# The bias stage of an attention and mixture kernel written into the one order of steps

## The chip, the cores and the metric

The kernel runs on one core of a Trainium2 chip. The metric is device time of one execution in microseconds (us). The core has five engines with a queue each: TensorE (PE, with its weight loads as PEld), VectorE (DVE), ScalarE (ACT), GpSimd (POOL) and SyncE (SP), which issues the transfers here. Each queue is worked off in order, and an instruction that waits holds up all that stand behind it on its engine.

## The reference, cut to what matters

Attention of 8 batches and 8 heads over 576 positions with 64 columns a head, with a bias that a small network makes of the positions, and then a soft mixture of 8 experts on what comes out:

```python
scores = scale * np.matmul(q, k.transpose(0, 1, 3, 2))
psi_rel = np.log1p(np.abs(pos[:, None] - pos[None, :]))
psi_i = np.log1p(np.maximum(pos[:, None], 1.0))
x = (psi_rel / psi_i)[..., None]
h = np.maximum(x @ w1 + b1, 0.0)          # 32 hidden units
scores = scores + (h @ w2).transpose(2, 0, 1)[None]
attn = softmax(scores);  out = np.matmul(attn, v)
# then a soft mixture: logits = out @ phi, softmax over tokens and over slots, 8 experts
```

The bias is the same for all batches: 576 x 576 values for each of 8 heads.

## The kernel before, in words

**The bias stage.** It comes first, and has 36 jobs (`jobs`), each for 16 rows of the bias and all heads. Job i needs four feature tiles f (128 partitions, 304 to 576 columns), each one instruction that scales a table and cuts it at zero: on DVE (line 324), but the first of the four on ACT in five jobs of six (line 321), so 114 on DVE and 30 on ACT. PE multiplies the four by the second layer's weights `wbd` side by side in the array (line 345), in pieces that meet at the diagonal and at a bank's end (three pieces, twelve products, in most jobs). ACT adds a constant and keeps the 591 columns as a tile e (line 349); SP stores e in DRAM (line 350, `bias_m`, and `bias_r` for the last four jobs). `bias_group()` writes one job, with the features of three jobs ahead (`AHEAD`), in the order of the row numbers. f and e tiles share 25 buffers (`W1N`, tag w); the PSUM banks are a fixed pair of four in turn. Then `load_bias` reads the bias of one pair of heads back, skewed, in five tiles (line 381): c = 0 to 3 need the stores of jobs 8c to 8c+7, and c = 4 (`br`, six transfers) those of jobs 32 to 35.

**The attention units.** A unit u is one pair of heads in one batch; there are 32. A unit has row blocks p (0 to 3, and 4 in even units for the rest rows of two units). The steps, by their names in the order: `Sp.n/u` are score products for both heads and one half of the columns (lines 465, and 470 for p = 4; two PSUM banks), `tp.hn/u` adds the bias and takes the running minimum on DVE (line 485, frees one bank), `ep.h/u` is the exponential on ACT (line 494), `mp` the reciprocal of the sums on DVE (lines 501, 502), `np.h` the division on POOL (line 400), `Tp` and `Rp` turn the result on PE (line 449), `cp` and `cRp` copy that out of PSUM (line 403; a plus sign after a name puts the copy on DVE, otherwise on ACT), `Mc` multiplies by v (line 571), `xc` copies that out, `xs` stores it, `lq`, `lv` and `b` load. Units 24 to 31 also hold the mixture's steps.

**The order.** `ORDER` is one written list of all steps of the units. `then` looks up each step's place, the steps are sorted by it, and each engine's queue is what the list gives it. PSUM banks of a step are the ones idle for longest at that place in the list (`Banks`). The bias stage isn't in the list of before: its calls stand ahead of it, and the compiler's own scheduler orders their transfers.

In the text, "the cut" is the place of `S0.0/5`, from which the lists of before and after are the same to the end.

Of the kernel before, what the change touches and what calls it, by code (L numbers as in the profile page):

```python
# [57 lines left out]
S1.0/8 S1.1/8 t1.10/8 n2.1/7 t1.00/8 R3/7 S3.0/8 t1.11/8 T2/7 cR3/7 xs/6 t1.01/8 e0.0/8 T3/7 t3.00/8 t3.10/8 m0/8
S3.1/8 c3/7+ xs/5 e1.0/8 e1.1/8 M0/7 m1/8 t3.01/8 S4.0/8 n0.1/8 c2/7 S4.1/8 e3.0/8 n0.0/8 t3.11/8 e3.1/8 x0/7+ t4.00/8
n1.0/8 t4.10/8 n1.1/8 R1/8 cR1/8 T0/8 t4.01/8 m3/8 n3.0/8 c0/8 t4.11/8 S2.0/8 lv/8 w0/8 e4.0/8 e4.1/8 S0.0/9 t2.10/8  # L60
t2.00/8 S2.1/8 S0.1/9 t2.11/8 t2.01/8 e2.1/8 w1/8 m4/8 n4.0/8 e2.0/8 n4.1/8 T1/8 n3.1/8 c1/8 M1/7 t0.00/9 R4/8 t0.10/9
T3/8 t0.11/9 t0.01/9 m2/8 cR4/8 e0.0/9 n2.1/8 T4/8 n2.0/8 x1/7+ S1.0/9 T2/8 c3/8+ c4/8 R3/8 S3.0/9 t1.00/9 t1.10/9
cR3/8+ c2/8 lq/10 S3.1/9 t3.00/9 t3.10/9 S1.1/9 S2.0/9 S2.1/9 t3.01/9 e0.1/9 t3.11/9 e3.1/9 M1/8 m0/9 n0.1/9 t2.10/9
e3.0/9 t2.00/9 t1.01/9 t1.11/9 e1.0/9 e1.1/9 lq/11 n0.0/9 t2.11/9 m3/9 e2.1/9 n3.0/9 m1/9 t2.01/9 n1.1/9 n1.0/9 n3.1/9
e2.0/9 M0/8 T0/9 x0/8 x1/8 m2/9 R1/9 S0.0/10 n2.0/9 S0.1/10 cR1/9 c0/9 t0.00/10 t0.10/10 T1/9 lv/9 w0/9 t0.01/10
# [4 lines left out]
e2.1/10 w1/10 m4/10 n4.0/10 e2.0/10 n4.1/10 T1/10 n3.1/10 c1/10 M1/9 t0.00/11 R4/10 t0.10/11 T3/10 t0.11/11 t0.01/11  # L70
m2/10 cR4/10 e0.0/11 n2.1/10 T4/10 n2.0/10 x1/9+ S1.0/11 T2/10 c3/10+ c4/10 R3/10 S3.0/11 t1.00/11 t1.10/11 cR3/10+
# [140 lines left out]
def body(ctx, tc, qk, v, wcol, phi, mw1, mw2, tabh, consth, out, outr):  # L212
# [95 lines left out]

    feats = {}

    def bias_feats(i):
        bases, scales, _ = jobs[i]
        fb = [None] * 4
        relu = [False] * 4
# [820 lines left out]
```

## Time and profile before

| what | us |
|---|---|
| runs | 597.39, 593.42, 595.76 (median 595.76) |
| profiled execution | 595.49 |
| its span, first to last instruction | 593.7 |
| around the span | 1.8 |

The profiled execution lies 0.27 us below the median, so a difference worked out in its trace is taken from its own time. The runs spread over 4 us. Times below count from the span's start. A busy share says how long an engine had something in flight; matmuls overlap, and their ends are modelled.

### The profile page before, as it was taken

How to read it: one execution, taken by the hardware profiler on the slowest of the kernel's cores; microseconds unless marked ns; L12 is line 12 of the kernel's file. 1: busy time of each engine (PE TensorE's matmuls, PEld its weight loads, DVE VectorE, ACT ScalarE, POOL GpSimd, SP SyncE). 2: the span in 40 equal slices, each digit the busy share in tenths (PEclk: the TensorE clock that was granted, in tenths of full speed). 3: DMA queues.
4: the chain of work that ended last, by engine and by line, in shares of the span. 5: the costliest groups of instructions: out<-in, count | busy, mean ns of one | idle time of the engine just before them, and what ended most of it. 6: DMA issues, size and time to landing. Idle time of an engine off the chain costs nothing.

```text
span 593.7 us, 19374 instructions
## 1 busy us (share of the span) xinstructions
PE 564.0 (95%) x7391; PEld 368.8 (62%) x7391; DVE 464.3 (78%) x1813; ACT 451.0 (76%) x954; POOL 259.4 (44%) x311
## 2 busy tenths in 40 slices
PE   6999799999999999999999999999999999999993
PEld 3875466666666666666666666667666666653551
DVE  7998698887787989888797989778888988652322
ACT  5996488897898898888888888788777887841333
POOL 5996354553545444544644454354335223400000
PEclk9999699999999999999999999999999999999998
DMA  6688332323764471858434243841433406499978
GB/s 212 245 296 290 99 107 83 90 85 99 210 241 177 136 263 56 303 173 305 150 127 172 94 146 105 277 165 66 131 121 118 153 33 216 141 400 410 408 319 319
DMA packets 43325, 111.94 MB, mean 189 GB/s; under 512 B 7904, under 2 KB 8032, under 8 KB 43232
## 3 DMA queue, kind: packets, MB, share of 16 engines
q1 hardware_dynamic: 43232, 110.71, 53.4%
q8 instruction: 58, 0.95, 0.7%
q14 instruction: 35, 0.29, 0.2%
HBM read 83.28 MB, written 27.41 MB: 186 GB/s over the span
## 4 chain that ended last, share of the span: by engine, by line
PE 73%; DVE 8%; DMA 6%; ACT 6%; issue 3%; POOL 2%; SPq 1%; POOLq 0%; DVEq 0%; ACTq 0%
PE ps L571 20%; PE ps L465 17%; PE ps L449 13%; PE ps L345 8%; DVE y L485 4%; ACT y L494 3%; PE ps L470 3%; PE ps L992 2%; PE ps L948 2%; POOL y L400 2%; ACT at L403 2%; DMA xs<-xts 1%; DVE sm L501 1%; PE ps L638 1%; PE ps L1025 1%
## 5 line engine op out<-in xcount | busy, mean ns | idle before, releaser
L400 POOL TENSOR_SCALAR y<-y,sm 128x576 f32<-128x576 f32 x288 | 211.4, 749 | 249.1 <-DVE sm L502 186.7
L494 ACT ACTIVATE y<-y,mn 128x576 f32<-128x576 f32 x288 | 221.0, 770 | 42.7 <-DVE mn L485 33.5
L571 PE MATMUL ps<-at,v 128*64 128x256 f32 (+1 forms) x1280 | 166.1, 410 | 0.7 <-DVE sm L502 0.4
L465 PE MATMUL ps<-qk 64*128 64x288 f32 x1024 | 154.6, 422 | 2.4 <-DVE mn L485 2.1
L403 ACT COPY at<-ps 128x1024 f32<-128x1024 f32 (+2 forms) x173 | 134.4, 793 | 27.0 <-PE ps L449 23.4
L571 PEld LDWEIGHTS ps<-at,v 128*64 128x64 f32 x1280 | 88.7, 137 | 67.8 <-DVE mn L485 7.2
L485 DVE CUSTOM_DVE_ANT_0 y<-ps,bm,mn 128x288 f32<-128x288 f32 x256 | 123.0, 512 | 6.9 <-PE ps L465 4.0
L485 DVE CUSTOM_DVE_ANT_0 y<-ps,bm 128x288 f32<-128x288 f32 x256 | 107.6, 454 | 21.5 <-PE ps L465 13.2
L449 PEld LDWEIGHTS ps<-ident,y 64*128 64x128 f32 x2592 | 97.8, 140 | 42.4 <-issue 16.5
L449 PE MATMUL ps<-ident,y 64*128 64x64 f32 x2592 | 110.3, 228 | 6.2 <-POOL y L400 2.5
L465 PEld LDWEIGHTS ps<-qk 64*128 64x128 f32 x1024 | 94.7, 189 | 23.6 <-DVE mn L485 5.2
L494 ACT ACTIVATION_READ_ACCUMULATOR y<-y,mn 128x1 f32 x288 | 54.5, 189 | 0.0
L501 DVE TENSOR_SCALAR sm<-sm 128x2 f32<-128x2 f32 x144 | 38.2, 265 | 19.1 <-ACT y L494 18.6
L345 PE MATMUL ps<-f,wbd 128*32 128x79 f32 (+30 forms) x856 | 48.4, 346 | 2.2 <-DVE f L324 2.1
L403 DVE COPY at<-ps 128x1024 f32<-128x1024 f32 (+2 forms) x51 | 42.7, 838 | 8.6 <-PE ps L449 7.0
L324 DVE TENSOR_SCALAR f<-tabs,scl,nb 128x576 f32<-128x576 f32 (+17 forms) x114 | 47.9, 501 | 0.9 <-DMA tabs<-in_tab_dram 0.9
L485 DVE DVE_READ_ACCUMULATOR2_ANT mn<- 128x1 f32 x576 | 47.8, 83 | 0.0
L282 POOL TENSOR_SCALAR phis<-phis 128x128 f32<-128x128 f32 x1 | 44.1, 44107 | 5.5 <-DMA phis<-in_moe_phi_dram 5.5
L345 PEld LDWEIGHTS ps<-f,wbd 128*32 128x32 f32 x856 | 33.3, 112 | 17.3 <-issue 7.5
L349 ACT ACTIVATE e<-ps,bcon 128x591 f32<-128x591 f32 x36 | 26.8, 752 | 4.4 <-PE ps L345 3.5
L502 DVE RECIPROCAL sm<-sm 128x2 f32<-128x2 f32 x144 | 23.9, 166 | 4.9
L470 PE MATMUL ps<-qk 64*64 64x288 f32 x256 | 23.5, 419 | 1.5 <-DMA qk<-in_qk_dram 1.3
(146 smaller groups left out, 382.2 us busy)
## 6 DMA issues: line engine op xcount, KB each, us to landing
wt<-in_moe_w_dram SPq DMA_DIRECT2D x62, 512.0 KB, 8.5
qk<-in_qk_dram SPq DMA_DIRECT2D x32, 608.0 KB, 4.6
v<-in_v_dram SPq DMA_DIRECT2D x32, 320.0 KB, 4.7
bias_m<-e SPq DMA_DIRECT2D x32, 295.5 KB, 4.4
out_dram<-ob SPq DMA_DIRECT2D x16, 512.0 KB, 4.7
xs<-xts SPq DMA_DIRECT2D x24, 288.0 KB, 4.5
xo<-xs SPq DMA_DIRECT2D x8, 864.0 KB, 4.7
bm<-bias_m SPq DMA_DIRECT2D x16, 288.0 KB, 3.7
```

Source lines behind the costliest of these rows:

```text
L282: nc.gpsimd.tensor_scalar(out=phis, in0=phis, scalar1=-1.0, scalar2=None, op0=ALU.mult)
L324: nc.vector.tensor_scalar(out=f, in0=tabs[:, 0:n], scalar1=scl[:, sc:sc + 1], scalar2=nb1[:, 0:1], op0=ALU.mult, op1=ALU.max)
L345: nc.tensor.matmul(pb[32 * t:32 * t + 32, c0 // 512, c0 % 512:(c1 - 1) % 512 + 1], wbd, x, start=True, stop=True, tile_position=(0, 32 * t))
L400: nc.gpsimd.tensor_scalar(out=out, in0=y, scalar1=r, scalar2=1.0, op0=ALU.mult, op1=ALU.mult)
L403: (nc.vector.tensor_copy if eng else nc.scalar.copy)(out=out, in_=in_)
L449: nc.tensor.matmul(out, src[rs], ident[rs, rs], is_transpose=True, start=True, stop=True, tile_position=(64 * r, 0))
L465: nc.tensor.matmul(pss[hh].t[:, 0:HALF], x[rs, 640 + p * P:640 + (p + 1) * P], x[rs, k0:k0 + HALF], start=True, stop=True, tile_position=( ...
L470: nc.tensor.matmul(pss[hh].t[64 * r:64 * r + 64, 0:HALF], x[rs, 1152:1216], x[rs, k0:k0 + HALF], start=True, stop=True, tile_position=(64 ...
L485: nc.vector.tensor_tensor_reduce(out=d["y", p][:, hs], in0=d["ps", p, n][hh].read()[:, 0:HALF], in1=biases[hp][p][:, hs], scale=-QS, scala ...
L494: nc.scalar.activation(out=y, in_=y, func=AF.Exp, bias=d["mn", p][:, 2 + hh:3 + hh], scale=-1.0, accum_out=d["sm", p][:, hh:hh + 1])
L501: nc.vector.tensor_scalar(out=r, in0=r, scalar1=1e-9, scalar2=None, op0=ALU.add)
L571: nc.tensor.matmul(po.t[64 * hh:64 * hh + 64, 0:w], d["v"][:, v0:v0 + 64], main[:, :, 4 * hh + i, :] if i < 4 else x[:, r0:r0 + w], start= ...
```

## The change

- Each of a job's steps is now a step of the list, under unit -1: `fi.t` (a feature; plus: on ACT, else DVE), `Bi` (its products), `Ei` (the kept row; plus: on DVE), `Di` (the store), and `bc` (a load of the first pair of heads' bias). The list before the cut has 611 names in place of 354; after it nothing is changed.
- The jobs no longer run by number: 13, 16, 19, 3, 10, 7, 5, 4 come first, 33 and 35 last. 37 features are on ACT and 107 on DVE; 35 rows are kept on ACT, one (E35) on DVE.
- `Bi` takes its banks by `Banks(2)`. The row is shifted in its two banks by `o0`, where it fits, so that the diagonal falls on the banks' border; the products are 320 in place of 428.
- `S0.0/0` stands between the features of job 25 and the products of job 22; `t0.10/0` and `t0.00/0` after B25 and B29; `S0.1/0`, `S1.0/0`, `S1.1/0`, `S2.0/0` among the last ten rows. The loads b0 to b4 stand one by one between the stores.
- The steps of units 0 to 4 stand in another order than before, and of their copies out of PSUM c are on ACT 20 times in place of 15, cR 3 in place of 10, x 5 in place of 3.
- `load_v(1)` stands ahead of `ready()`, which loads and negates phi on POOL.

```diff
+    def bias_job(i):
+        bases, scales, dst = jobs[i]
+        n = max(bases[0] + 16, S - bases[0])
+        i0 = bases[0] + 16
+        o0 = 512 - i0 if 0 <= 512 - i0 and S + 15 - i0 <= 512 else 0
+        d, fb, relu = {}, [None] * 4, [False] * 4
+
+        def feats(eng, t):
+            f = fb[t] = wp.tile([P, S], F32, name="f", tag="w")[:, 0:n]
+            sc = scl[:, scales[t]:scales[t] + 1]
+            relu[t] = eng
+            if eng:
+                nc.scalar.activation(out=f, in_=tabs[:, 0:n], func=AF.Relu, bias=cols[:, 1:2], scale=sc)
+            else:
+                nc.vector.tensor_scalar(out=f, in0=tabs[:, 0:n], scalar1=sc, scalar2=nb1[:, 0:1], op0=ALU.mult, op1=ALU.max)
+
+        def products(_):
+            pb = d["pb"] = Banks(2)
+            cuts = sorted({0, i0, 512 - o0, S + 15})
+            for c0, c1 in zip(cuts, cuts[1:]):
+                a = c0 + o0
+                for t in (1, 2, 3, 0):
+                    x = fb[t][:, i0 - c1:i0 - c0][:, ::-1] if c0 < i0 else fb[t][:, c0 - i0 + 1:c1 - i0 + 1]
+                    nc.tensor.matmul(pb.t[32 * t:32 * t + 32, a // 512, a % 512:a % 512 + c1 - c0], wbd, x, start=True,
+                                     stop=True, tile_position=(0, 32 * t))
+
+        def keep(eng):
+            e = d["e"] = wp.tile([P, S + 15], F32, name="e", tag="w")
+            k = 1 * relu[0] + 2 * relu[3]
+            x = d["pb"].read().rearrange("a x n -> a (x n)")[:, o0:o0 + S + 15]
+            if eng:
+                nc.vector.tensor_scalar(out=e, in0=x, scalar1=bcon[:, k:k + 1], scalar2=None, op0=ALU.add)
+            else:
+                nc.scalar.activation(out=e, in_=x, func=AF.Identity, bias=bcon[:, k:k + 1])
+        for t in range(4):
+            step(-1, f"f{i}.{t}", lambda eng, t=t: feats(eng, t))
+        step(-1, f"B{i}", products)
+        step(-1, f"E{i}", keep)
+        step(-1, f"D{i}", lambda _: nc.sync.dma_start(out=dst, in_=d["e"]))
     load_qk(0)
     load_v(0)
-    for j in range(4):
-        bias_group()
     load_qk(1)
+    load_v(1)
     ready()
-    for j in range(JB0):
-        bias_group()
-    load_v(1)
+    for i in range(len(jobs)):
+        bias_job(i)
     for c in range(5):
-        load_bias(0, c)
+        step(-1, f"b{c}", lambda _, c=c: load_bias(0, c))
```

The list of after, from its start, and around the last rows (names of unit -1 without it):

```
f2.2 f13.0+ f13.3 f3.0 f10.3+ f16.2 f3.1 f13.1 f13.2 f16.1 f16.3+ f16.0+ f7.3+ f5.0+ f19.1 f7.1 B13 ...
... E18 f9.3+ D4 f12.2 f21.2 f12.0+ f8.0 B11 f12.3 f9.0 E6 f12.1 B0 D7 ...
... f33.2 D30 f32.0+ f35.3 D27 B32 f35.1 f35.0+ b2 S2.0/0 E34 f33.0+ e0.0/0 E32 e0.1/0 t1.01/0 B33 E33 B35
t1.11/0 m0/0 n0.1/0 S2.1/0 D34 t2.10/0 E35+ S3.0/0 t2.11/0 b3 e1.0/0 e1.1/0 D32 n0.0/0 T0/0 D33 t2.00/0 m1/0
e2.1/0 t2.01/0 c0/0 e2.0/0 S3.1/0 t3.00/0 t3.10/0 n1.1/0 n1.0/0 t3.01/0 t3.11/0 S0.0/1 S0.1/1 R1/0 m2/0 e3.0/0
T1/0 cR1/0+ t0.00/1 D35 n2.1/0 t0.10/1 t0.01/1 b4 c1/0 t0.11/1 e3.1/0 S4.0/0 e0.1/1 S4.1/0 lq/2 m3/0 n2.0/0
T2/0 M0/0 e0.0/1 t4.00/0 c2/0 t4.01/0 e4.0/0 t4.10/0 m0/1 n3.0/0 n3.1/0 t4.11/0 R3/0 e4.1/0 n0.1/1 S1.0/1 x0/0
cR3/0+ t1.10/1 t1.00/1 n0.0/1 m4/0 b1/7 S1.1/1 T3/0 ...
```

## Rows read from the trace of the kernel before

**Rows 1.** The page's head and busy times: engine, busy us, share, instructions.

```profile
span 593.7 us, 19374 instructions
PE 564.0 (95%) x7391; PEld 368.8 (62%) x7391; DVE 464.3 (78%) x1813; ACT 451.0 (76%) x954; POOL 259.4 (44%) x311
```

**Rows 2.** Busy time by windows: stretch, length, engines' busy us (instructions), PE clock, DMA.

```profile
5.30:54.40 49.10, 48.36 (x858) 33.32 (x858) 47.87 (x114) 44.41 (x66) 44.11 (x1) 1.00 0.75 266
...
54.40:62.50 8.10, 5.88 (x48) 3.31 (x44) 4.83 (x23) 3.90 (x9) 0.69 (x1) 1.00 0.74 249
62.50:72.80 10.30, 8.10 (x56) 5.68 (x57) 6.86 (x31) 5.78 (x13) 4.38 (x7) 0.50 0.25 63
...
82.50:125.70 43.20, 42.98 (x564) 29.32 (x562) 37.58 (x163) 37.82 (x83) 22.67 (x31) 1.00 0.31 96
```

**Rows 3.** Groups by line from 5.3 to 54.4 us: busy us, mean ns | idle before.

```profile
L349 ACT ACTIVATE e<-ps,bcon 128x591 f32<-128x591 f32 x35 | 26.1, 752 | 3.1 <-PE ps L345 2.2 <-DMA bias_m<-e 0.6
L321 ACT ACTIVATE f<-tabs,cols,scl 128x560 f32<-128x560 f32 (+17 forms) x30 | 22.3, 751 | 0.4 <-DMA bias_m<-e 0.3
L324 DVE TENSOR_SCALAR f<-tabs,scl,nb 128x576 f32<-128x576 f32 (+17 forms) x114 | 47.9, 501 | 0.9 <-DMA tabs<-in_tab_dram 0.9
```

**Rows 4.** Timeline of PE from 54 us on: start, us, instructions merged [idle before].

```profile
54.38 2.70 PE L465 MATMUL ps<-qk 64*128 64x288 f32 x20
...
61.41 1.92 PE L465 MATMUL ps<-qk 64*128 64x288 f32 x4 [2.13 <-DVE mn L485]
...
65.63 0.37 PE L449 MATMUL ps<-ident,y 64*128 64x64 f32 x1 [1.38 <-DVE mn L485]
66.74 1.99 PE L449 MATMUL ps<-ident,y 64*128 64x64 f32 x19 [0.74 <-DVE mn L485]
...
114.82 1.33 PE L470 MATMUL ps<-qk 64*64 64x288 f32 x16
...
124.57 1.27 PE L449 MATMUL ps<-ident,y 64*128 64x64 f32 x34
125.68 1.19 PE L465 MATMUL ps<-qk 64*128 64x288 f32 x8
...
127.50 2.31 PE L465 MATMUL ps<-qk 64*128 64x288 f32 x16
129.74 5.07 PE L571 MATMUL ps<-at,v 128*64 128x256 f32 x40
134.75 1.34 PE L449 MATMUL ps<-ident,y 64*128 64x64 f32 x36
```

**Rows 5.** The chain that ended last, around the last bias row: start, us, what.

```profile
54.58 0.76 ACT e L349
55.36 4.80 DMA bias_r<-e
...
63.34 2.72 DMA br<-bias_r
```

**Rows 6.** Timeline of DVE, ACT and POOL: start, us, instruction [idle before].

```profile
9.48 44.11 POOL L282 TENSOR_SCALAR phis<-phis 128x128 f32<-128x128 f32 x1 [5.49 <-DMA phis<-in_moe_phi_dram]
...
58.46 0.76 ACT L494 ACTIVATE y<-y,mn 128x576 f32<-128x576 f32 x1
...
65.11 0.46 DVE L485 CUSTOM_DVE_ANT_0 y<-ps,br 128x288 f32<-128x288 f32 x1 [1.61 <-DMA br<-bias_r]
...
66.60 0.52 DVE L485 CUSTOM_DVE_ANT_0 y<-ps,br,mn 128x288 f32<-128x288 f32 x1
...
67.04 0.51 DVE L485 CUSTOM_DVE_ANT_0 y<-ps,br,mn 128x288 f32<-128x288 f32 x1
...
75.82 1.01 ACT L403 COPY at<-ps 128x1024 f32<-128x1024 f32 x1 [0.74 <-PE ps L449]
```

**Rows 7.** Waits from 5 to 54 us, ACT on stores: us, times, longest.

```profile
ACT e L349 <- DMA bias_m<-e: 0.6, 1, 0.6
ACT f L321 <- DMA bias_m<-e: 0.3, 1, 0.3
```

More of the change, by code (lines that the diff above doesn't have):

```diff
@@ new lines @@
+D23/-1 f22.2/-1 E0/-1 f26.3/-1 f14.0/-1 E11/-1 B21/-1 B12/-1 B14/-1 f31.2/-1 f8.1/-1 E21/-1 f9.1/-1 f22.0/-1 E12/-1
+f20.0/-1+ f20.3/-1+ f30.1/-1 E14/-1 B9/-1 D18/-1 E9/-1 f22.3/-1 f22.1/-1 f8.2/-1 D6/-1 f25.0/-1+ f26.2/-1 f8.3/-1
+f25.1/-1 S0.0/0 f31.0/-1+ f31.3/-1 B22/-1 f20.2/-1 E22/-1 B8/-1 f31.1/-1 B20/-1 D0/-1 f24.3/-1 f24.2/-1 E8/-1 D11/-1
+f27.1/-1 B31/-1 f24.0/-1+ f24.1/-1 f26.1/-1 f25.3/-1 f26.0/-1+ E20/-1 f28.1/-1 f28.3/-1 f28.2/-1 D12/-1 f25.2/-1
+B24/-1 D21/-1 E31/-1 D14/-1 f29.2/-1 f28.0/-1+ f30.2/-1 B26/-1 B28/-1 f29.1/-1 E24/-1 f29.3/-1 b0/-1 E26/-1 f30.0/-1
@@ new lines @@
+D9/-1 f29.0/-1+ f27.2/-1 f30.3/-1+ f27.3/-1 D8/-1 E28/-1 B25/-1 B29/-1 D22/-1 t0.10/0 t0.00/0 B30/-1 f32.2/-1 D20/-1
+f27.0/-1+ D31/-1 f34.2/-1 E29/-1 f33.1/-1 E25/-1 E30/-1 B27/-1 b1/-1 f34.3/-1 S0.1/0 E27/-1 f34.0/-1 f34.1/-1 D26/-1
+t0.11/0 f32.3/-1+ t0.01/0 S1.0/0 f32.1/-1 S1.1/0 D24/-1 D28/-1 t1.10/0 B34/-1 t1.00/0 D29/-1 f33.3/-1 D25/-1 f35.2/-1
+f33.2/-1 D30/-1 f32.0/-1+ f35.3/-1 D27/-1 B32/-1 f35.1/-1 f35.0/-1+ b2/-1 S2.0/0 E34/-1 f33.0/-1+ e0.0/0 E32/-1 e0.1/0
+t1.01/0 B33/-1 E33/-1 B35/-1 t1.11/0 m0/0 n0.1/0 S2.1/0 D34/-1 t2.10/0 E35/-1+ S3.0/0 t2.11/0 b3/-1 e1.0/0 e1.1/0
@@ L307, in body @@
     nc.vector.memset(bcon[96:128, 2:4], 0.0)
[L309 to L314, printed above, removed]
-        for t in range(4):
-            sc = scales[t]
-            n = max(bases[0] + 16, S - bases[0])
-            f = fb[t] = wp.tile([P, S], F32, name="f", tag="w")[:, 0:n]
-            relu[t] = t == 0 and i % 6 != 5
-            if relu[t]:
-                nc.scalar.activation(out=f, in_=tabs[:, 0:n], func=AF.Relu, bias=cols[:, 1:2],
-                                     scale=scl[:, sc:sc + 1])
-            else:
-                nc.vector.tensor_scalar(out=f, in0=tabs[:, 0:n], scalar1=scl[:, sc:sc + 1], scalar2=nb1[:, 0:1],
-                                        op0=ALU.mult, op1=ALU.max)
-        feats[i] = fb, relu
-    nb = [0]
-    def bias_group():
-        i = nb[0]
-        nb[0] += 1
-        for j in range(i if i else 0, i + AHEAD + 1):
-            if j < len(jobs) and j not in feats:
-                bias_feats(j)
-        bases, scales, dst = jobs[i]
-        fb, relu = feats[i]
-        pb = ps(i % 4)
-        i0 = bases[0] + 16
-        cuts = sorted({0, i0, 512, S + 15})
-        for c0, c1 in zip(cuts, cuts[1:]):
-            for t in (1, 2, 3, 0):
-                x = fb[t][:, i0 - c1:i0 - c0][:, ::-1] if c0 < i0 else fb[t][:, c0 - i0 + 1:c1 - i0 + 1]
-                nc.tensor.matmul(pb[32 * t:32 * t + 32, c0 // 512, c0 % 512:(c1 - 1) % 512 + 1], wbd, x, start=True,
-                                 stop=True, tile_position=(0, 32 * t))
-        e = wp.tile([P, S + 15], F32, name="e", tag="w")
-        bc = bcon[:, 1 * relu[0] + 2 * relu[3]:1 * relu[0] + 2 * relu[3] + 1]
-        nc.scalar.activation(out=e, in_=pb.rearrange("a x n -> a (x n)")[:, 0:S + 15], func=AF.Identity, bias=bc)
-        nc.sync.dma_start(out=dst, in_=e)
     jobs = []
```

320 lines of the change are left out of this document (163 added, 157 removed).

## The prediction

> **What bounds the kernel now.** The page first: PE is in flight for 95% of the span [rows 1], so the question is where PE loses time that the change can touch. The list is the same from the cut on, and PE comes to the cut at 125.68 us: there it runs the two score steps of unit 5, just behind 34 half turns that end unit 4 [rows 4]. So the prediction is when PE will reach the cut; what lies behind it moves along.
>
> The windows show two stages ahead of it [rows 2]. In the bias stage (5.3 to 54.4 us) DVE works 47.87 of 49.10 us and ACT 44.41. PE shows 48.36, but it is fed row by row: a score step puts 288 columns through for both heads in 0.56 us (2.24 us from one row to the next for four steps, [rows 4]), so the 591 columns of a bias row are worth some 1.15 us, 41 us for 36. The stage is bound by making features and rows, not by PE. Its last products end at 54.38 us, when the scores begin.
>
> In the second stage (54.38 to 125.68 us, 71.3 us) PE is the bound but loses time. Its work there, from pitches [rows 4]: 42 score steps at 0.56 = 23.5; six of the block p = 4 at 0.67 = 4.0 (16 instructions in 1.33); 394 half turns at 1.11/34 = 12.9; eight products with v at 5.01/2 = 20.0; in all 60.4 us. The same rates give 42.2 us for the full window from 82.5 to 125.7 us (104, 32, 304 instructions and six products), which took 43.2 [rows 2], so I scale by 1.023: 61.8. Some 9.5 us are lost. Idle rows hold 2.13 + 1.38 + 0.74 = 4.25 of them [rows 4]; most of the rest lies in 62.5 to 72.8 us, where the granted clock is 0.50, the lower of its two levels (1.2 GHz), behind a window in which PE worked 5.88 of 8.10 us [rows 2].
>
> What makes PE wait there is in the chain [rows 5]: the last row is kept at 54.58 to 55.34 us, its store lands only 4.80 us after its issue, the six loads of br follow, and the last loads take 2.72 us more. The first addition of block 4 runs at 65.11 us, released by that load [rows 6]: 9.8 us after the row was ready. DVE, ACT and PE stand in written order behind it.
>
> **The change part by part.**
>
> *Features and rows.* Seven features go from DVE to ACT. DVE: 107 at 47.9/114 = 0.42 [rows 3] is 44.9 us. ACT: one feature is 0.60 (busy time left beside 35 rows of 0.752) to 0.75 us [rows 3], so 44.41 + 7 x 0.7 = 49.3 us for 37 features and 35 rows (the window of before holds 35 rows as well). So ACT becomes the stage's bound. Its last feature, f33.0, has two rows behind it (1.5 us): 5.4 + 49.3 - 1.5 = 53.2 us if ACT never waits. Before, it idled some 4 us in the stage [rows 2, 3]; work from many jobs is at hand now, so I take 2 between 0 and 4: 55.2 us. DVE is earlier: with six additions at 0.44 (the pitch from 66.60 to 67.04, [rows 6]) it has written its last feature at 5.3 + 44.9 + 2.6 = 52.8. Then B33 and B35 at 1.15 each: the last products end at **57.5 us**, 3.1 later than before.
>
> *Products cut at the diagonal.* 108 fewer products, the same columns. PE has some 8 us to spare in the stage, so I cost it at nothing; without that cover it would be a gain, at most 108 x 0.03 = 3 us (a half turn's pitch for the smallest piece).
>
> *Scores between the last rows.* Five score steps (2.8 us of PE) are done before B35, inside PE's spare time, and seven additions and a few exponentials with them. After B35 PE has 61.8 - 2.8 = 59.0 us to the cut. S0.0/0 keeps two of eight banks for some ten jobs; three pairs for a row in turn, with 1.15 us of products and 0.75 of keeping, are enough for a row every 1.4 us, so this is at nothing too.
>
> *Stores and loads.* The same bytes. b0, b1 and b2 stand between the stores, eight or more jobs behind the rows that they read, so the additions of blocks 0 to 2 find them landed; b3 has D24 to D31 long ahead of it. The 2.13 us ahead of block 3 goes. b4 cannot go early: it needs D35, and E35 now stands on DVE behind B35 and one addition. E35 costs what it did on ACT, 0.75, and ends at 58.2. From there the chain of before holds [rows 5, 6]: 9.8 us to t4.00, **68.0 us**; the second half of the load came 1.1 us later before, so t4.11 ends near 70.0. Queued behind t4.00 on DVE are the additions of unit 1, and behind them PE: S1.0/1 takes a bank that t4.00 frees and S1.1/1 one of t4.11, and PE works in order. Meanwhile PE has five score steps (2.8), two of block 4 (1.3), three turns (1.6), R1 (0.1) and M0/0 (2.5), 8.3 us, to 65.8; then R3 and S1.0/1 (0.7). It stands idle for some 3.5 us between 65.8 and 70.0.
>
> Here the Trainium skill gives another price: DMA: Bandwidth & Descriptors, in "Anatomy of one DMA", has a fixed cost of about 2.0 us for a transfer, so store and load would be some 4 us. The row has 4.80 us for the store alone [rows 5], with 0.74 of the DMA engines' time taken in that window [rows 2]; the measurement decides. By the page, as an estimate, t4.00 could run at about 65 us, PE would not stand, and the cut would come near 116.5 us, the time of the rival "hidden" below.
>
> *Copies in units 0 to 4.* Five c copies go to ACT at 1.01 us [rows 6] and seven small cR copies to DVE. ACT's work to the cut is then 47 exponentials at 0.76, 20 copies at 1.01, and small ones (some 2.3): 58 us, of which two exponentials are done early. That is 56.5 us in the 62.5 from 57.5 to the cut: 90%, where ACT ran at 37.82 of 43.2 (88%) before [rows 2]. So ACT is close to PE but not ahead of it; nothing is added for it, and 0 to 2 us go into the range.
>
> *POOL.* The negation of phi takes 44.11 us and ends at 53.59 [rows 6], as DVE's features end. The first division stands behind it in POOL's queue, but also behind every DVE feature through its own inputs, so this costs nothing; if additions also held it up, each us would come straight onto T0.
>
> **The sum.** From 70.0 us PE has 59.0 - 8.3 - 0.7 = 50.0 us to the cut: 120.0 us in place of 125.68, 5.7 us less. The profiled execution took 595.49 us, 1.8 of them around the span, so **589.8 us**; against the median of 595.76 that is 1.0%. The bounds of what the trace does not show (ACT's waits 0 to 4 us, the chain 7.5 to 12, ACT's share 0 to 2) make it 586 to 592.5.
>
> **The rivals.**
>
> *Hidden.* ACT waits less and the last store lands sooner, as fewer transfers are in flight: B35 ends near 55.5, PE finds work until t4.00 comes. Then the cut is 55.5 + 59.0 = 114.5 to 116.5: **585.5 us**. For it: br's additions are the only ones that must wait. Against it: the 4.80 us row, and the job order ends on the bias_r rows as before. Chance 0.2.
>
> *The clock falls again.* The 3.5 us in which PE stands are longer than the 2.13 that preceded the low clock before [rows 4], and M0 and the turns ahead of them are light. A stretch like that of before costs what is left of the 9.5 us lost: 9.5 - 4.25 = 5.2 less what ACT hides, some 4: cut at 124, **593.8 us**. The Trainium skill says in TensorE: Matmul & The Clock Gate, "HAM oscillation", that waits on transfers bring the gate back each time; the trace shows it once, at 62.5 us [rows 2]. Against it: in the 8 us ahead PE is fuller than the 5.88 of 8.10 before. Chance 0.23.
>
> *Slots.* The 25 buffers of f and e are all taken at three places of the new list; f8.0 follows D4 by four names and f31.3 D6 by seven. With the slot longest free taken, 26 writes take the slot of a store. Where a store is really issued only near its place in the list, such a write stands for its landing, 4.80 us. Two whole ones and one us for each of the others are 9.6 + 24 = 33.6 us on DVE and ACT together, 17 on each, less the 2.4 by which DVE is early: last products near 72 us, the wait for b4 behind them hidden in part, cut near 132 to 134, **603 us**, slower by over 1%. It decides from about 6 us of such waits on one engine (slower than before at all), 12 for 1%. Against it: before, with the same 25 buffers, ACT waited 0.6 + 0.3 us for stores in all [rows 7], and DVE never [rows 3]; SP can issue as soon as a row is kept, well before the place in the list. Chance 0.10.
>
> *Nothing.* DVE's additions only displace features, and the saved waits return at b4: cut at 124 to 126, 594 to 595.8. Chance 0.05.
>
> **How the numbers follow.** My forecast has 0.42. A measurement of this kernel tells a change from none at about 1%, 5.96 us; faster by over that is below 589.8, where my forecast stands just at the edge. Faster: hidden 0.2 and a good half of the forecast, 0.46. Slower by over 1% (above 601.7): most of the slots' case, 0.08. Same: 0.46. Range: down to hidden with the shorter chain, 584.5; up over the clock's case to no gain, 596; that leaves out the slots and a little below.
>
> **What would show it.** Right: PE's first score product in the bias stage, near 45 us; the last products near 57.5; a load of br behind the last store, t4.00 released by it at 68, and one PE idle stretch there of 2 to 4 us; no idle row ahead of block 3; the cut near 120. Wrong: DVE or ACT waiting on bias_m stores for more than 3 us; a clock of 0.50 in any stretch before the cut; ACT with no idle time from 57 us on while PE waits for its copies; or a cut moved without the end moving.

## The result, and the profile after

The changed kernel takes 589.68 us (median of four runs, 586.38 to 591.13), the kernel before 594.86 us beside it: ratio 0.990, 95% interval 0.9859 to 0.9941. The profiled execution took 590.42 us with a span of 588.6. A second set of runs of the same kernel (after_again, below) gave 591.14 us and 0.9934 (0.9909 to 0.9959). So the change is worth 0.4 to 1.4%, and the forecast of 589.8 us stands. Of the executions in the table further down one, late4b's of 599.45 us, is a slow one (over 1.5% above that kernel's fastest) and is left out of its ratio.

The page's head and busy times of the changed kernel, to be read against [rows 1]:

```profile
span 588.6 us, 18890 instructions
PE 557.2 (95%) x7175; PEld 356.9 (61%) x7175; DVE 458.9 (78%) x1807; ACT 456.5 (78%) x960; POOL 215.4 (37%) x311
```

PE's share is the same. POOL is 44.0 us lighter, which nothing in the diff explains (last section).

The same windows as in [rows 2], and one more from the last bias product to the cut:

```profile
5.30:54.40 49.10, 44.97 (x662) 22.64 (x664) 47.59 (x124) 49.09 (x78) 1.13 (x2) 1.00 0.76 272
54.40:62.50 8.10, 7.39 (x92) 4.82 (x93) 6.85 (x32) 6.80 (x15) 4.24 (x6) 1.00 0.60 207
62.50:72.80 10.30, 9.19 (x80) 6.71 (x78) 6.18 (x29) 6.45 (x15) 4.39 (x6) 0.83 0.51 161
...
54.28:119.58 65.30, 63.16 (x751) 43.30 (x752) 51.65 (x235) 55.25 (x116) 32.76 (x45) 0.97 0.34 106
```

ACT never rests in the bias stage (49.09 of 49.10 us; 44.41 before), and PE has 44.97 us of work there with 22 score instructions in it. From 62.5 to 72.8 us the granted clock is 0.83 on average, where it was 0.50.

The groups by line from 5.3 to 54.4 us, to be read against [rows 3]:

```profile
L877 DVE TENSOR_SCALAR f<-tabs,scl,nb 128x368 f32<-128x368 f32 (+17 forms) x106 | 44.7, 496 | 1.1 <-PE ps L886 0.8 <-DMA bias_m<-e 0.2
...
L875 ACT ACTIVATE f<-tabs,cols,scl 128x416 f32<-128x416 f32 (+17 forms) x37 | 27.0, 791 | 0.0
L896 ACT ACTIVATE e<-ps,bcon 128x591 f32<-128x591 f32 x35 | 25.1, 784 | 0.0
```

Neither engine waits for a store in any way that counts: DVE 0.2 us, ACT nothing. So the 25 buffers of f and e are enough.

PE's timeline around the last rows and at the cut, to be read against [rows 4]:

```profile
51.66 2.63 PE L886 MATMUL ps<-f,wbd 128*32 128x512 f32 x48
54.21 0.76 PE L438 MATMUL ps<-qk 64*128 64x288 f32 x4
55.60 0.76 PE L438 MATMUL ps<-qk 64*128 64x288 f32 x4 [0.63 <-DVE mn L458]
...
56.96 2.37 PE L438 MATMUL ps<-qk 64*128 64x288 f32 x12
59.16 1.03 PE L422 MATMUL ps<-ident,y 64*128 64x64 f32 x20
...
64.65 0.70 PE L438 MATMUL ps<-qk 64*128 64x288 f32 x2
66.09 1.42 PE L438 MATMUL ps<-qk 64*128 64x288 f32 x4 [0.74 <-DVE mn L458]
67.88 0.67 PE L438 MATMUL ps<-qk 64*128 64x288 f32 x1 [0.37 <-DVE mn L458]
...
118.47 1.28 PE L422 MATMUL ps<-ident,y 64*128 64x64 f32 x34
119.58 1.19 PE L438 MATMUL ps<-qk 64*128 64x288 f32 x8
```

The last bias products end at 54.28 us. The cut is the x8 row behind the 34 half turns: 119.58 us, 125.68 before. Of the idle rows ahead of it [rows 4] the 2.13 and the 1.38 are gone. The cut moved by 6.10 us and the span by 5.1.

The chain that ended last, around the last row, to be read against [rows 5]:

```profile
56.31 4.08 DMA bias_r<-e
63.82 2.68 DMA br<-bias_r
```

Timelines of POOL, DVE and SP, to be read against [rows 6]:

```profile
10.54 0.96 POOL L298 TENSOR_SCALAR phis<-phis 128x128 f32<-128x128 f32 x1 [6.54 <-DMA phis<-in_moe_phi_dram]
...
55.08 0.46 DVE L458 CUSTOM_DVE_ANT_0 y<-ps,bm 128x288 f32<-128x288 f32 x1 [1.01 <-PE ps L438]
...
55.46 0.83 DVE L894 TENSOR_SCALAR e<-ps,bcon 128x591 f32<-128x591 f32 x1
...
65.57 0.46 DVE L458 CUSTOM_DVE_ANT_0 y<-ps,br 128x288 f32<-128x288 f32 x1 [3.15 <-DMA br<-bias_r]
...
54.60 2.03 SPq L902 DMA_DIRECT2D bias_r<-e  x3
60.48 3.94 SPq L354 DMA_DIRECT2D br<-bias_r  x6
```

Read it as one path: the last row (E35) is kept at 55.46 to 56.29 us, its store is one of SP's three and lands 4.08 us after its issue, SP issues the six loads of br from 60.48 to 64.42, and t4.00 runs at 65.57, when the fourth of them has landed (65.41; the sixth lands at 66.50). That wait, 3.15 us, is the longest that DVE has between the stage and the cut.

### The profile page after: what moved, and what is told of

Its sections match the earlier page's. It is cut to its first block, busy times and chain, and to the rows that moved or that the text cites. A ratio compares the mean times of both kernels' runs of the same rounds, so it can differ in the third digit from the quotient of the medians.

```text
span 588.6 us, 18890 instructions
## 1 busy us (share of the span) xinstructions
PE 557.2 (95%) x7175; PEld 356.9 (61%) x7175; DVE 458.9 (78%) x1807; ACT 456.5 (78%) x960; POOL 215.4 (37%) x311
## 4 chain that ended last, share of the span: by engine, by line
PE 62%; DVE 12%; ACT 8%; DMA 7%; issue 5%; SPq 2%; POOL 2%; DVEq 0%; POOLq 0%; ACTq 0%
PE ps L544 17%; PE ps L438 15%; PE ps L422 12%; DVE y L458 6%; ACT y L467 3%; PE ps L443 3%; PE ps L1005 2%; PE ps L961 2%; DMA bm<-bias_m 2%; DMA xs<-xts 2%; PE ps L886 2%; POOL y L373 2%; SPq L354 2%; ACT e L896 2%; PE ps L611 2%
## 5 line engine op out<-in xcount | busy, mean ns | idle before, releaser
L376 ACT COPY at<-ps 128x1024 f32<-128x1024 f32 (+2 forms) x171 | 137.2, 817 | 27.7 <-PE ps L422 22.1
L438 PE MATMUL ps<-qk 64*128 64x288 f32 x1024 | 156.3, 422 | 1.9 <-DVE mn L458 1.7
L886 PE MATMUL ps<-f,wbd 128*32 128x512 f32 (+49 forms) x640 | 42.0, 400 | 5.6 <-DVE f L877 3.3
L877 DVE TENSOR_SCALAR f<-tabs,scl,nb 128x560 f32<-128x560 f32 (+17 forms) x107 | 45.2, 496 | 1.4 <-PE ps L886 0.8
L376 DVE COPY at<-ps 128x256 f32<-128x256 f32 (+2 forms) x53 | 39.4, 743 | 8.3 <-PE ps L422 6.5
L886 PEld LDWEIGHTS ps<-f,wbd 128*32 128x32 f32 x640 | 20.8, 112 | 26.8 <-issue 9.3
L875 ACT ACTIVATE f<-tabs,cols,scl 128x416 f32<-128x416 f32 (+17 forms) x37 | 27.0, 791 | 0.0
L896 ACT ACTIVATE e<-ps,bcon 128x591 f32<-128x591 f32 x35 | 25.1, 784 | 0.0
## 6 DMA issues: line engine op xcount, KB each, us to landing
bias_m<-e SPq DMA_DIRECT2D x32, 295.5 KB, 3.6
```

What stands on the lines that cost most here:

```text
L376: (nc.vector.tensor_copy if eng else nc.scalar.copy)(out=out, in_=in_)
L438: nc.tensor.matmul(pss[hh].t[:, 0:HALF], x[rs, 640 + p * P:640 + (p + 1) * P], x[rs, k0:k0 + HALF], start=True, stop=True, tile_position=( ...
L877: nc.vector.tensor_scalar(out=f, in0=tabs[:, 0:n], scalar1=sc, scalar2=nb1[:, 0:1], op0=ALU.mult, op1=ALU.max)
L886: nc.tensor.matmul(pb.t[32 * t:32 * t + 32, a // 512, a % 512:a % 512 + c1 - c0], wbd, x, start=True, stop=True, tile_position=(0, 32 * t))
L896: nc.scalar.activation(out=e, in_=x, func=AF.Identity, bias=bcon[:, k:k + 1])
```

## The experiments

Theory A: what counts is the chain from the last row through its store and its load to t4.00, and how much other work the written order puts ahead of t4.00. Scores among the last rows only move the place where PE waits. Theory B: the scores among the last rows are the gain, as they give PE 2.8 us of work that it would else do later. Medians are of 6 to 12 executions (the changed kernel: 4), in five batches that each had the kernel before beside them, so kernels of different batches are compared by their ratios. The cut and the row of t4.00 are from one profiled execution each; the half clock is the time at a granted clock of 0.50 ahead of the cut.

| kernel | median us | ratio to before, 95% | t4.00 at (its wait) | half clock, us | cut, us |
|---|---|---|---|---|---|
| changed | 589.68 | 0.990, 0.9859 to 0.9941 | 65.57 (3.15) | 3.41 | 119.58 |
| after_again | 591.14 | 0.9934, 0.9909 to 0.9959 | 69.25 (3.77) | 6.83 | 124.18 |
| no_overlap | 591.12 | 0.9937, 0.9912 to 0.9961 | 66.81 (1.22) | none | 120.15 |
| old_stage | 590.63 | 0.9917, 0.9888 to 0.9946 | 65.70 (none) | none | 119.36 |
| old_units | 598.36 | 1.007, 1.0037 to 1.0102 | 66.80 (5.55) | 10.24 | 126.73 |
| old_cuts | 590.25 | 0.9925, 0.9898 to 0.9952 | 66.88 (3.30) | 3.41 | 121.35 |
| late4b | 596.89 | 1.0024, 0.9996 to 1.0052 | 70.77 (none) | 3.41 + 6.83 | 126.36 |
| br_free | 590.96 | 0.9943, 0.9921 to 0.9964 | 67.83 (none) | 3.41 | 121.42 |
| br_early_rows | 585.60 | 0.9852, 0.9807 to 0.9898 | 65.15 (none) | none | 118.68 |
| swap34 | 590.23 | 0.9902, 0.9867 to 0.9936 | (block 4 ahead of block 3) | 6.83 | 122.81 |
| br_order | 589.88 | 0.9901, 0.9863 to 0.9939 | 66.09 (1.55) | none | 119.91 |
| e35_first | 590.51 | 0.9902, 0.9867 to 0.9937 | 67.49 (2.19) | 3.41 | 122.23 |
| pool_loads | 592.57 | 0.9957, 0.9931 to 0.9983 | 69.64 (none) | 10.24 | 125.01 |

**The same kernel again (after_again).** No edit.

> The changed kernel once more, beside the others on one chip. Both theories: about 0.99 of the kernel before, some 589.5 us; in the trace the last products near 54 us, the first addition of block 4 near 65.6 us released by the load of br, the cut near 119.6 us.

Its profiled execution has the same wait with another size: the last products end at 55.94 us, 1.7 later, and DVE stands longer.

```profile
69.25 0.46 DVE L458 CUSTOM_DVE_ANT_0 y<-ps,br 128x288 f32<-128x288 f32 x1 [3.77 <-DMA br<-bias_r]
```

The cut is 4.6 us later than in the first profile of the same kernel. A cut read from one execution can be off by that much, so verdicts go by the intervals, and the traces show only where time is lost.

**All bias steps ahead of the first score (no_overlap).** The list keeps the order of the bias steps and that of the unit steps, but no score stands among the rows.

```diff
-f25.1/-1 S0.0/0 f31.0/-1+ f31.3/-1 B22/-1 f20.2/-1 E22/-1 B8/-1 f31.1/-1 B20/-1 D0/-1 f24.3/-1 f24.2/-1 E8/-1 D11/-1
...
+f33.0/-1+ E32/-1 B33/-1 E33/-1 B35/-1 D34/-1 E35/-1+ b3/-1 D32/-1 D33/-1 D35/-1 b4/-1 S0.0/0 t0.10/0 t0.00/0 S0.1/0
```

> The changed kernel with every bias step ahead of the first score product, all else in its order. Theory A (what counts is the time from the last row to block 4 and how much work of the units lies between them): the last row comes some 1.5 to 2 us earlier, as two exponentials and seven additions no longer stand ahead of it, so br lands near 64 us; DVE then has 20 additions and four sums, about 10.6 us, ahead of block 4, more than the 9.3 us from the last row to br, so DVE's wait of 3.2 us for br goes, and the end moves by less than 1.5 us either way (588 to 591 us). Theory B (the scores between the last rows bring the gain): PE has five score steps more behind the last row, 2.8 us, and the end is 2.8 us or more later: 592.3 us or above.

591.12 us, 0.9937 (0.9912 to 0.9961), as the changed kernel beside it (after_again, 0.9934). Its last products end at 53.76, and t4.00 waits 1.22 us instead of 3.15:

```profile
66.81 0.46 DVE L457 CUSTOM_DVE_ANT_0 y<-ps,br 128x288 f32<-128x288 f32 x1 [1.22 <-DMA br<-bias_r]
```

```profile
56.25 4.61 DMA bias_r<-e
```

The last row is kept earlier, by 54.71 us, as theory A has it, but br lands no earlier than before: the row's store stands behind the loads of b3 and two other stores in SP's queue and is issued at 56.25 only. Theory B falls: its 592.3 us lies just above the interval (592.0 at most). A loss of less than some 2 us couldn't be told from none. What PE has done early it lacks when br is late.

**The stage of before with the new order of the units (old_stage).** Job by job as before, features and rows on the engines of before, b0 to b4 ahead of the scores, and units 0 to 4 as in the changed list.

```diff
+D32/-1 B33/-1 E33/-1 D33/-1 B34/-1 E34/-1 D34/-1 B35/-1 E35/-1 D35/-1 b3/-1 b4/-1 S0.0/0 t0.10/0 t0.00/0 S0.1/0
```

> The bias stage in the order of before (jobs by number, the same features on ACT, all rows kept on ACT, no score product ahead of its end), behind it the units in the order of the changed kernel. Theory A (the units' order, with block 4 late, and the loads early bring the gain, not the stage): DVE has 20 additions, some 10 us, ahead of block 4, more than the time from the last row to br; block 4 does not wait by more than 1 us, the cut comes near 121 us, 590 to 592 us. Theory B (the stage's job order and the scores in it bring the gain): 593.5 us or more, near the kernel before.

590.63 us, 0.9917 (0.9888 to 0.9946): the gain is there without the new stage. The addition of block 4 and the window that was at 0.50 before:

```profile
65.70 0.46 DVE L457 CUSTOM_DVE_ANT_0 y<-ps,br 128x288 f32<-128x288 f32 x1
```

```profile
62.50:72.80 10.30, 10.09 (x144) 6.93 (x140) 8.89 (x44) 9.73 (x23) 5.88 (x8) 1.00 0.35 119
```

No wait for br stands on the row, and PE is busy for 10.09 of 10.30 us at full clock, against 8.10 at half [rows 2]. But br comes earlier here too. SP's loads of br in the kernel before and here, and the windows from 52 to 56 us (before, here; the last two numbers are the DMA engines' share and GB/s):

```profile
60.23 3.70 SPq L381 DMA_DIRECT2D br<-bias_r  x6
56.93 3.70 SPq L353 DMA_DIRECT2D br<-bias_r  x6
```

```profile
52.00:56.00 4.00, 4.00 (x48) 2.44 (x46) 2.02 (x8) 1.51 (x2) 1.58 (x1) 1.00 1.03 386
52.00:56.00 4.00, 4.00 (x42) 2.71 (x42) 1.88 (x9) 1.41 (x2) 0.96 (x1) 1.00 0.50 197
```

The last row is kept by 54.70 us, its store lands 2.12 us after its issue where it took 4.80 before, and the load that t4.00 needs lands at 61.68, four us ahead of t4.00. So this kernel shows that the new stage isn't needed for the gain, but not whether the later place of block 4 or the earlier br brings it: the order of before with so early a br was not run.

**The new stage with the old order of the units (old_units).** The stage of no_overlap, then units 0 to 4 in the order of before.

```diff
-t2.11/0 e1.0/0 e1.1/0 n0.0/0 T0/0 t2.00/0 m1/0 e2.1/0 t2.01/0 c0/0 e2.0/0 S3.1/0 t3.00/0 t3.10/0 n1.1/0 n1.0/0 t3.01/0
+S3.1/0 e1.1/0 n0.0/0 n0.1/0 t3.01/0 t3.11/0 S4.1/0 m1/0 t4.00/0 t4.10/0 n1.0/0 e3.1/0 S2.0/0 e3.0/0 t4.01/0 t4.11/0
```

> The bias stage's steps in the order of the changed kernel, all ahead of the units, and units 0 to 4 in the order of the kernel before, where block 4 stands behind 12 additions. Theory A: the last row is kept near 54.7 us, br lands near 64, DVE reaches block 4 near 60.5 and waits 3 to 4 us, PE behind it, as before; 592.5 to 595 us. Theory B: the gain of the changed kernel stays, 589 to 591 us.

598.36 us, 1.007 (1.0037 to 1.0102): the gain is lost, and the time is above theory A's range too. Here t4.00 stands behind 12 additions (blocks 0, 1 and 3), in the new order behind 20 (blocks 0 to 3, and block 0 of unit 1). DVE, PE and the window:

```profile
66.80 0.46 DVE L458 CUSTOM_DVE_ANT_0 y<-ps,br 128x288 f32<-128x288 f32 x1 [5.55 <-DMA br<-bias_r]
```

```profile
67.32 0.37 PE L422 MATMUL ps<-ident,y 64*128 64x64 f32 x1 [5.58 <-DVE mn L458]
68.49 1.99 PE L422 MATMUL ps<-ident,y 64*128 64x64 f32 x19 [0.80 <-DVE mn L458]
```

```profile
62.50:72.80 10.30, 4.61 (x32) 3.56 (x32) 4.29 (x16) 2.93 (x8) 1.55 (x3) 0.53 0.21 59
```

```profile
56.95 4.91 DMA bias_r<-e
```

DVE comes to t4.00 some 5.5 us before br, PE stops behind it, and 10.24 us at half clock follow. Against no_overlap, which has the same steps of the stage in the same order, the cut is 6.6 us later, and the intervals lie apart. The row is kept by 54.89 us and its store issued at 56.95, again late in SP's queue, so br comes as in no_overlap: t4.00 runs at 66.80 and 66.81. So on the new stage it is the order of units 0 to 4 that carries the gain. The engines of their copies changed with it; the two were not tested apart. The new stage with the old order is slower than the kernel before, where the store was issued at 55.36 [rows 5].

**The cuts at the diagonal taken back (old_cuts).**

```diff
-        o0 = 512 - i0 if 0 <= 512 - i0 and S + 15 - i0 <= 512 else 0
+        o0 = 0
```

> The changed kernel with the rows not shifted in their banks (428 products in place of 320). Both theories: PE has time to spare in the stage, so within 1 us of the changed kernel; if the smaller products do cost, at most 3 us more (593 us).

590.25 us, 0.9925 (0.9898 to 0.9952). The interval overlaps both of the changed kernel's: no price of the 108 products is to be seen, as costed.

**Block 4 still later (late4b).** The block goes behind six additions of unit 1.

```diff
-S0.0/1 S0.1/1 R1/0 m2/0 e3.0/0 T1/0 cR1/0+ t0.00/1 D35/-1 n2.1/0 t0.10/1 t0.01/1 b4/-1 c1/0 t0.11/1 e3.1/0 S4.0/0
...
+S2.0/1 t1.01/1 t1.11/1 c3/0 t2.00/1 t2.10/1 S4.0/0 e1.0/1 e1.1/1 S4.1/0 lq/2 b1/7 t4.00/0 t4.01/0 m1/1 e4.0/0 t4.10/0
```

> The changed kernel with the four additions of block 4 of unit 0 and what hangs on them moved behind six additions of unit 1 (2.7 us of DVE work). Theory A: the wait for br is filled with them, DVE's wait falls from 3.2 us to under 1, and the end is 1.5 to 3.5 us earlier, 586 to 588 us. Theory B: no change within 1 us, as the wait is covered, or slower, as the load of the next q waits for block 4's products.

A miss: 596.89 us, 1.0024 (0.9996 to 1.0052). The wait for br is gone, but others stand in its place:

```profile
67.71 0.46 DVE L458 CUSTOM_DVE_ANT_0 y<-ps,bm 128x288 f32<-128x288 f32 x1 [2.38 <-PE ps L422]
```

```profile
76.52 1.22 PE L422 MATMUL ps<-ident,y 64*128 64x64 f32 x18 [2.89 <-POOL y L373]
```

An addition of unit 1 waits for a turn of PE, and later PE for a division on POOL. More work ahead of the wait had a price here; that it is the buffers of y, which two units then hold at once, is an argument and was not tested. Theory B's reason isn't in the trace: the load of the next q is issued at 71.63 us (64.46 in the changed kernel), but no wait up to the cut is put down to it.

**br without the last row's store (br_free, br_early_rows).** Both read br from rows of block 0, kept long before; br_free also issues b4 behind b1.

```diff
+        if n == 64 and h < 2:
+            (row, k), (head, _), _ = bias_m[0].ap
+            x = bass.AP(bias_m[0].tensor, bias_m[0].offset + head * h + k - 1 + j0, [[row - 1, n], [1, j1 - j0]])
+            nc.sync.dma_start(out=out, in_=x)
+            return
```

> The changed kernel, but the first pair of heads reads its bias of block 4 from rows stored early (those of block 0), and its load stands behind b1; the bias of those rows is left out of the output. Theory A: block 4 waits for nothing, DVE's 3.2 us of waiting at 62 to 65.6 us go, PE's short idle rows there too and with them the clock's fall behind them; 2 to 4 us faster than the changed kernel, 585.5 to 587.5 us. Theory B: the wait is covered by ACT's and PE's other work, same as the changed kernel within 1 us.

A miss, and a muddled test: 590.96 us, 0.9943 (0.9921 to 0.9964). The six early issues keep SP busy, and the stores and b2's load that stand behind them come late. t4.00 waits for nothing, but block 2 does:

```profile
59.14 0.46 DVE L463 CUSTOM_DVE_ANT_0 y<-ps,bm 128x288 f32<-128x288 f32 x1 [4.55 <-DMA bm<-bias_m]
```

So it was tried again with every step in its place:

> The changed kernel with every step in its place, but the first pair of heads reads its bias of block 4 from rows of block 0, stored long before; the right bias of those rows is left out of the output. This takes the landing of the last store (4.1 us in the trace of the changed kernel) out of the path to block 4 and moves no load. Theory A (the last store's landing sets when block 4 runs): br lands near 62 us, DVE's wait of 3.2 us falls under 1 us, 2 to 4 us faster than the changed kernel (586 to 588 us). Theory B (the wait is covered by ACT and PE): within 1 us of the changed kernel.

585.60 us, 0.9852 (0.9807 to 0.9898), the only kernel whose interval lies wholly below that of after_again. SP issues the loads from 58.28 us, not from 60.48, and no stretch at half clock stands ahead of the cut:

```profile
65.15 0.46 DVE L463 CUSTOM_DVE_ANT_0 y<-ps,br 128x288 f32<-128x288 f32 x1
```

```profile
62.50:72.80 10.30, 10.20 (x143) 6.96 (x137) 9.22 (x46) 9.47 (x20) 5.90 (x8) 1.00 0.45 144
```

By the ratios, taking the last row's landing out of the path is worth 0.5 to 0.8%, 3 to 5 us, against the two sets of runs of the changed kernel, which is what theory A asks for; the interval overlaps that of the first set. The traces don't show the size. The fourth load lands at 64.44 us, not near 62, and DVE comes to t4.00 at 65.15 instead of 62.42, after waits of 1.32, 0.65 and 0.26 us for b2 and b3. The cut comes 0.9 us ahead of the changed kernel's first profile and 5.5 ahead of after_again's; against the first, the other 2.8 us of the span lie behind the cut, where the list is the same. The kernel adds other rows' biases, so it is no version to keep.

**Block 4's rows ahead of block 3's (swap34).** Jobs 32 to 35 change places with 26, 28, 25 and 29, b3 with b4, and blocks 3 and 4 of unit 0.

```diff
-t1.01/0 B33/-1 E33/-1 B35/-1 t1.11/0 m0/0 n0.1/0 S2.1/0 D34/-1 t2.10/0 E35/-1+ S3.0/0 t2.11/0 b3/-1 e1.0/0 e1.1/0
+t1.01/0 B25/-1 E25/-1 B29/-1 t1.11/0 m0/0 n0.1/0 S2.1/0 D26/-1 t2.10/0 E29/-1+ S4.0/0 t2.11/0 b4/-1 e1.0/0 e1.1/0
```

> The changed kernel with the jobs of block 4 (32 to 35) in the places of jobs 26, 28, 25 and 29 and those in the last four places, the loads b3 and b4 exchanged, and in unit 0 the steps of blocks 3 and 4 exchanged. The last row then belongs to block 3, whose first addition needs one load of three and not the fourth of six. If the chain from the last row sets the end: 4.1 us of landing, 0.5 of issue and 2.7 of the load, 7.3 in place of 9.3 us, DVE's wait ahead of the late block falls from 3.2 to about 1.2 us, and the end is 1 to 3 us earlier than that of the changed kernel (587 to 589.5 us). If not: within 1 us of it.

590.23 us, 0.9902 (0.9867 to 0.9936): no better. The first addition of block 2 waits for b2, and the last row (E29) is kept on DVE behind it:

```profile
58.11 0.46 DVE L458 CUSTOM_DVE_ANT_0 y<-ps,bm 128x288 f32<-128x288 f32 x1 [3.03 <-DMA bm<-bias_m]
58.49 0.83 DVE L894 TENSOR_SCALAR e<-ps,bcon 128x591 f32<-128x591 f32 x1
```

**The loads of br in another order (br_order), the last row earlier on DVE (e35_first), two loads on POOL's queue (pool_loads).** The three build on one another.

```diff
-            for r in range(2):
-                rs = slice(64 * r, 64 * r + 64)
+            both = [slice(64 * r, 64 * r + 64) for r in range(2)]
+            for rs in both:
                 read_bias(x[rs, 0:S], bias_r, h0, 0, S)
...
-t1.01/0 B33/-1 E33/-1 B35/-1 t1.11/0 m0/0 n0.1/0 S2.1/0 D34/-1 t2.10/0 E35/-1+ S3.0/0 t2.11/0 b3/-1 e1.0/0 e1.1/0
+t1.01/0 B33/-1 E33/-1 B35/-1 E35/-1+ t1.11/0 m0/0 n0.1/0 S2.1/0 D34/-1 t2.10/0 S3.0/0 t2.11/0 b3/-1 e1.0/0 e1.1/0
...
+            eng = nc.gpsimd if hp == 0 and c in (2, 3) else None
```

> The changed kernel with the six loads of br in another order: both halves of the rows for the first head, then for the second. The first addition of block 4 needs the first and the second load in place of the first and the fourth, 1.2 us of issue less. If the chain from the last row sets the end: 0.5 to 1.5 us earlier than the changed kernel (589 to 590.5 us by the same batch). If not: no change.

589.88 us, 0.9901 (0.9863 to 0.9939). t4.00 waits 1.55 us and the other head's first addition 0.74 more. That is less than 3.15 in one, but not a time that can be told from the changed kernel's.

> The six loads of the first head's bias rows as in br_order, and the last row's exponential on VectorE moved right behind the masks' row B35, ahead of the turns of unit 1 that wait for a load. If the chain from the last row's end through its store and its load sets the first addition of block 4, the row ends earlier and the time is 0.5 to 2 us under br_order, 588 to 589.5, with no wait over 0.5 us at the first addition of block 4. Rival: SyncE is busy issuing loads and the other stores until about 57.8 us, so the store starts no earlier than before and the time is that of br_order, 589.5 to 591.

590.51 us, 0.9902 (0.9867 to 0.9937): the rival held. E35 ends at 56.42 (57.99 in br_order), but SP issues three loads first and the last three stores at the old time (56.74 to 58.33 in br_order):

```profile
55.30 1.27 SPq L354 DMA_DIRECT2D bm<-bias_m  x3
56.61 1.68 SPq L904 DMA_DIRECT2D bias_r<-e  x3
63.21 4.37 SPq L354 DMA_DIRECT2D br<-bias_r  x6
```

The store then takes 5.51 us to land, and t4.00 still waits 2.19 us, where theory A had 0.5 at most. Its row names PE as what ended the wait, but the load that it needs, the second, lands at 67.33, 0.16 us ahead of it:

```profile
57.62 5.51 DMA bias_r<-e
```

```profile
67.49 0.46 DVE L460 CUSTOM_DVE_ANT_0 y<-ps,br 128x288 f32<-128x288 f32 x1 [2.19 <-PE ps L546]
```

> As e35_first, with the loads of the second and third bias blocks of the first pair issued from GpSimd's queue, so that SyncE is free for the last rows' stores. If the last row's chain sets the end: the store is issued right behind the row, the bias rows land near 63 us, the first addition of block 4 waits for nothing, and the time is 586 to 588.5. Rival: the loads issued from GpSimd land later or hold GpSimd's additions up, blocks 2 or 3 wait on VectorE, and the time is 590 or more.

592.57 us, 0.9957 (0.9931 to 0.9983): the rival again. SP has issued the last stores by 57.02 and t4.00 waits for nothing, but b3 stands on POOL behind the first division, which waits for its inputs until 57.57, and block 3 waits on DVE, 2.10 and 2.74 us:

```profile
57.57 0.74 POOL L376 TENSOR_SCALAR y<-y,sm 128x576 f32<-128x576 f32 x1 [10.03 <-DVE sm L478]
58.27 1.65 POOL L354 DMA_DIRECT2D bm<-bias_m  x3
```

```profile
64.86 0.46 DVE L461 CUSTOM_DVE_ANT_0 y<-ps,bm 128x288 f32<-128x288 f32 x1 [2.74 <-DMA bm<-bias_m]
```

A queue that is free of SP's stores has its own written order; a wait was exchanged for another.

## Why the prediction was right

The mechanism and the place hold: the wait at block 3 goes, the wait for br stays at t4.00, and the cut comes near 120 us (119.58). Several of the terms were off, and they cancel, so that the forecast comes within 0.4 us of this cut and 0.1 us of this median is luck: the second set of runs of the same kernel gave 591.14 us, and its profile a cut at 124.18.

- *Last products at 57.5 us: 54.28.* The 2 us for ACT's waits were not there: ACT idled for 0.01 us of 49.10, and it did three exponentials beside 37 features and 35 rows in the time that I gave to features and rows alone: its last feature was done near 51.2 us, where I had 53.2 without any wait. That ACT becomes the stage's bound was right; 0 was the better end of my 0 to 4.
- *The chain, 9.8 us: 9.28* (56.29 to 65.57), with 4.08 us for the store where [rows 5] have 4.80. The Trainium skill has a fixed cost of about 2.0 us for a transfer in DMA: Bandwidth & Descriptors, "Anatomy of one DMA", which that section gives for transfers that GpSimd issues; both of these rows, issued by SP, are above it. In old_stage the same store took 2.12 us, so the chain is no constant, and 9.8 was a good price for this kernel and not for that one (7.0).
- *t4.00 at 68.0 us: 65.57.* The row was kept 1.9 us earlier than I had it (56.29 for 58.2) and not 3.2, as t2.10, ahead of it on DVE, waited 1.01 us for the products of S2.1; the rest is the shorter chain.
- *PE idle for some 3.5 us before t4.11 ends: 0.74 + 0.37 us*, and 0.63 ahead of it at 55.60. The steps of PE between the last products and the wait reach to 65.35 (64.65 + 0.70), 11.1 us with the 0.63; I had put them at 8.3 + 0.7. So PE came to the wait with less to lose, and the one idle stretch of 2 to 4 us that I had named as a sign isn't there.
- *No low clock: 3.41 us of it*, from 68.10 to 71.51, behind those waits. As the clock is halved, 1.7 us is the most that it can cost. An estimate from rows: 12 score instructions take 2.20 us from 56.96 us on, and 34 half turns 1.11 [rows 4], so the 13 and 16 that PE does from 68.22 to 71.92 us are 2.9 us of work, and 0.8 are lost. I had named a low clock ahead of the cut as a sign against the forecast. It is the rival "the clock falls again" in a small form; after_again has 6.83 us of it and a cut at 124.18, that rival's own 124, though its median is 591.14 and not 593.8 (its profiled execution took 592.99). So the forecast and this rival are two sizes of one wait.
- *59.0 us of PE's work behind the last row: 63.16 busy* in 65.3 us. With 0.8 to 1.7 for the clock 2.5 to 3.4 us remain that the pitches of [rows 4] did not hold; 1.4 of them lie ahead of the wait (11.1 less 0.63, for 9.0). What they are was not taken apart. In all: the last products 3.2 us earlier, PE's busy time 4.2 longer, its idle time 2.1 in place of 3.5, and the cut 0.4 ahead of 120.0.
- *Scores between the last rows, costed as 2.8 us of PE's time: nothing that could be told.* This is the step whose reason failed, though the sum did not need it: the 50.0 us behind 70.0 are the same with these scores done later, as they would only have filled most of the 3.5 us in which PE stands. no_overlap has the same time: as long as t4.00 waits for br, work that PE has done early is missing where it waits.
- *The order of units 0 to 4* is what the gain hangs on. The prediction had it in the work that it lists between the last row and t4.00 but gave it no term. old_units loses the gain with the new stage, and old_stage keeps it with the stage of before, though with an earlier br. That it is the place of block 4, behind 20 additions and not 12, is what the waits of 5.55 us (old_units) against 1.22 (no_overlap) speak for; the block's place alone, with every other unit step as before, was not tried.
- *Products cut, copies, POOL's negation: nothing*, as costed (old_cuts; ACT 55.25 of 65.3 us busy up to the cut, 85%).
- *The signs.* The first score product runs at 33.8 us, not 45; no idle row is left that waits for block 3's bias (the 0.63 us ahead of S3.0 are a wait for a bank); the load of br behind the last store releases t4.00, as said.
- *Slots: excluded.* DVE waited for a bias store 0.2 us, ACT never.
- *What lies behind the cut moves along:* to within about 1 us here. From the cut to the span's end 468.0 us before, 469.0 after, and 465.1 to 470.4 in the other kernels, with the same list there.

## What to carry to other kernels

When a result goes out to memory and back, find the first instruction that needs it and count the work that the written order puts ahead of it: here 20 additions instead of 12 cover nearly the whole of a chain of 9 to 12 us, and with them it hardly mattered which stage stood ahead (0.9917 with the old one, 0.990 to 0.9937 with the new). Take the chain from the kernel that is to run: a late place in SP's queue made it longer in old_units, and in old_stage it was 7 us. Filling an earlier stage with later work gained nothing while that wait stood, and pushing the consumer too far back brought other waits. Moving a step on the queue that issues the transfers, or to another queue, exchanges one wait for the next unless all that stands ahead of it there is counted.

## What the runs showed of the hardware

The negation of phi, one 128x128 instruction on POOL, took 44.11 us before [rows 6] and 0.96 us after, with the same shape and line. In the other kernels with the new order of the jobs it took 0.74 to 2.00 us, and in old_stage, with the order of before, 42.72. So it goes with the order of the stage's steps (and with it which features are ACT's), not with the instruction; DVE runs features back to back beside it in both, and what lets POOL through was not tested. It had no price in either, since nothing needs phi until later.

PE's low clock came ahead of the cut in stretches of 3.41, 6.83 or 10.24 us, beside or behind PE's waits for additions and divisions there, and not in every kernel that had such waits: br_order, with 1.55 us of DVE's time at t4.00, had none. The changed kernel has another 3.41 us at 382.13 us, where the list is that of before; its cause is open, and it may be part of the 1 us that the stretch behind the cut lost.

The store of the last row, 295.5 KB, landed 4.80 us after its issue before, 4.08 after, 5.51 in e35_first and 2.12 in old_stage. Where it took 2.12 the DMA engines were busy for 0.50 of the time from 52 to 56 us, where it took 4.80 for 1.03 (a mean share of the 16 engines, which can come out a little over 1). No run changed the traffic alone, so that this is the cause is not shown.
